# Attention into a gated feed-forward chain on one core: softmax sums turned once and spread by way of DRAM, last keys in one product

## The chip, the cores and the metric

The kernel runs on one core of one Trainium2 chip. The metric is the device time of one execution in microseconds. The time given is the median of several executions, and one further execution was profiled.

## The reference

```
scores = q @ k^T / sqrt(64)                   # 4 batches, 8 heads, 576 keys and queries, width 64
thresh = max(scores) - tau
scores = where(scores >= thresh, scores, -1e9)
attn   = exp(scores - max); attn /= sum(attn) + 1e-9
x      = attn @ v, heads side by side          # 2304 x 512
x      = (sigmoid(x @ w_gate) * (x @ w_val)) @ w_out      # 512 -> 1536 -> 512
h      = x @ w_in; out = (h * cos(h)) @ w_out2            # 512 -> 2048 -> 512
```

All in float32. Products are made on TensorE in float32r from a rounded high part and a rest, three matmuls (high by high, high by low, low by high) for one product.

## The kernel before

**Tiling.** Two heads make a pair; there are 16 pairs, four for each batch. A pair has nine score tiles of 128 queries by 576 keys: four for each head (`order`, line 566), and one that holds the last 64 queries of both heads. For one tile (`Queries.tasks`, line 589, with the key letters of the order lines): S, the scores on TensorE; M, the extreme of each row on VectorE (line 690); Y, the threshold, one column on VectorE (`threshold`, line 572); E, the exponential on ScalarE; K, the mask on VectorE, which also adds up each row into one column of the pair's `sums` tile (line 698); T, four 128x128 transposes to put keys on partitions (line 710), and t, one transpose for the last 64 keys of both heads (line 718). Each transposed tile is then split for the value product: H or h copies the rounded high part out of PSUM on ScalarE, and L or l takes the rest on VectorE (`low`, line 650); the table `LOWS` may give the rest to GpSimd by way of a copy (C, G) or to TensorE by a subtraction (N, n) and ScalarE (O, o).

**Value products.** `Values` (line 723) has four tasks V for each pair, two blocks of queries (256 and 320 columns) by two heads. The weights hold the high and low half of v side by side, so that 128 columns of weights give both. Each takes ten matmuls: high and low for four chunks of 128 keys, and high and low for the last keys, `LT`, which has both heads on its partitions (line 765). A "shared" one takes fifteen and needs no folding. The others are folded: F copies half of the result on ScalarE, A adds it into `x32` on VectorE.

**The sums.** `finish_pair` (line 779): p adds 1e-9 to the nine columns of `sums` (ScalarE), I inverts them (VectorE). For each of two blocks, R spreads four columns over 256 columns on GpSimd (`widen`), B transposes them on TensorE, two or three transposes of 128 columns (`spread`, line 806), so that each partition gets the factors of its head along the queries, and U multiplies x by them on VectorE from PSUM (`scaled`, line 815), with two more of 64x64 in the second block.

**After that.** D stores x to DRAM, X and x split it for the feed-forward stage (lines 839 and 840), and P are the first feed-forward products of batches 0 to 2 for half of the inner width (`groups`, line 863); their results are copied (e) to one of three `st` tiles and stored (g). They fill TensorE between the attention's tasks.

**Order.** The table `ORDER` gives a line of letters for each engine, in which each letter takes the next task of its kind; each engine's queue runs in that order. `WHERE` says on which engine some kinds run for each pair. The feed-forward stage that follows is laid out by the planner (`Plan.put_out`) without a table.

Of the kernel before, what the change touches and what calls it, by code (L numbers as in the profile page):

```python
# [19 lines left out]
P = 128  # L20
# [6 lines left out]
NT = 9  # L27
# [35 lines left out]
    ACT=(
        "JZQJQQwEEH6EHhEswHQOEh6HEFwCEHHHFhhEsHhEOQHEOpHh6EOEwaHHCE6FHZEOwhhEoo6HEFHHwHCEhhEHFhopEHHEOOh6wHEEsaHEF6HE"
        "OhhwoHEHHHEFZeHhh6EFHhEpOEHheewOEEFC6HFHwZEHeEhOXeh6EHEaHHehHEFhHEepwheHHEOhe6EHwEeHC6aEEFHChEHheEeHHHQFHEhF"
        "hEHpheEHheCHEEeFHCEFCsHhEhECHeeHHHEEFhhHpFHEheheECHEeEHFHCEEFHZehOEEHCheHHHEhhHFpeHEhEhFeHEEeFHCHEEFHChheEEH"
        "CeFHHCHEEHhhFpeHhEhECHeFHCHEFEZHChEEheHCeHHHEFhEhHehFpHEHehEEeHFCHEFEHChheEHEZFHHHEehhCHEeFhHphECEHeeHEEFCHF"
        "CHEhhEeHCEHHHEFhhHCeEhHEpFHhECEeFHHEFECHhhEEHCHHXHeEhhEHhpeFHCEEHhFeHECEHFCFEHhhEeHCeEHHHEehhEHFhpFHECheHEEe"
        "HFHCEFHEChEheEHZeHHHEeEhHFhhpFHEHehEHEeCHFEaEHChhEHCEFeHCHHEhheEHFhHEephECHeEEHCFHeEEFHChECHhEeHHHFHEhhehHbp"
        "FHheFFXeX"  # L70
    ),
    DVE=(
        "jzqjqqMYM4KY5KMLMYYKLlKM45YMlKYLKMAYMKLYLl4lKMYMKlY5AKMlIYMYKK4U5MLYMKAYUMK4Y5MKYLKMAYM4YLLKllKLMYMIYA5KKlMU"
        "YMKYLK4M5LYAMUKYlKM4YLMKYLLLKA5MlLYlKMAlMIYYKKlMYM45YKAUKMAYLMUYK45KlMlMLYKYKLMLYlLMAKlYLKIlM4Y5LKlMYUMYK4K5"
        "LMYMYKKAUMlYMKLlYKLLLMMYAYLlKlALlMIYKKlMUMYLKYMAYKAKUMMYlYKKlMYMLLYLKKlALAMIYlLKlMYlKMUYMYKKLAMYMYKKAUMYlMYK"
        "KlMYLLLKMLAlYlMLlKYlIKAMLYMYUKKALMMYYKKAUMlMlYKYKMAYMLYLKKLllAMLIlMlYUKYKAMLYMYKAKUMMlYYKKlMMLLLYKYlAlKLMIlA"
        "YLKMLlMUYYKKLMAYMKAYUKMllMYYKLKAMLLYLMYKllKlALMIMYlYKKMYUMYLKKAMAUMYYlKKlMMYYKLLLKAllMMYlYKKLILMlAYMYKUKMALY"
        "MKAYUKMlMYlKYKMLLMYLKYllKLIlMAMLYYKKlMAUMYKYKAMAYULMlYKlKMMYYKLLLMYKllLKAMlYALKIlMYMKYUKLAMMYKYAUKMYlMKlYKLM"
        "MYYLLLKKLllAMIlAYLKMLlMYYKUKLMYMAYKUKlMlMYYKKAMLLYMllKYLKMALYlMIYlKKUMYMKYKLAMMYYKKAUMlYMYKlKLLLMAYLllKLlIAL"
        "lAUAUx"  # L80
    ),
    POOL=(
        "ZJ7jqz7cGJjqR7RGs7Xx7zcJQqRGj7R7XxcJzjQR7RqG7x7zscJjQRq7R7sGXZGcxzqJRjGRGZGzGcXJjxQRqGRGscGJzXxQqRjsRGcGXxZG"
        "QzGqRJGRjGGzXxJcGRsQqRjGGscQqGzRRJGGjGcsGZGQqRJzRGZjGscGQXxxXJRqGRGxzjGXscGZxzQJqRGRGcsGjRQJzRqGjGZcGGRRzGGc"
        "GGRRXxXxx"
    ),
# [193 lines left out]
def pool1(n):  # L280
    return 0.03 + n / 943
# [1202 lines left out]
```

## Time and profile before

| what | us |
|---|---|
| median of 3 runs | 1146.27 |
| lowest and highest | 1146.10, 1146.92 |
| profiled execution, own time | 1143.7 |
| its span, first to last instruction | 1141.9 |

TensorE is busy for 97% of the span, VectorE 78%, ScalarE 62%, GpSimd 35%. The attention stage ends on TensorE with the last product L393 before 415.40 us, where the first product of the feed-forward stage begins. The page's slices say how busy an engine is; whether it waits is read from the windows and waits.

### The profile page before, as it was taken

Reading aid. Unit: us, or ns where it says so; the run is one execution under the profiler, and the core shown is the slowest. Engines: PE = TensorE matmul, PEld = TensorE weight load, DVE = VectorE, ACT = ScalarE, POOL = GpSimd, SP = SyncE. Lnnn points to the kernel's source line nnn. Section 1 sums busy time; section 2 is a strip of 40 time slices with the busy share of each in tenths; the row PEclk is TensorE's granted clock in tenths of the full one; section 3 lists DMA queues with packets and bytes.
Section 4 is the critical chain, followed back from the end, with each engine's and each line's share of the span. In section 5 each row is a group of like instructions: output and inputs, shape, how many; then the busy total and the mean of one; then the engine's idle time right before and its main releaser. Section 6 shows DMA issues by size and latency. Waiting matters only on the chain. (4 is left out here: it accounts for less than half of the span.)

```text
span 1141.9 us, 17082 instructions
## 1 busy us (share of the span) xinstructions
PE 1110.0 (97%) x5986; PEld 951.7 (83%) x5986; DVE 889.4 (78%) x1691; ACT 709.4 (62%) x1322; POOL 403.3 (35%) x338
## 2 busy tenths in 40 slices
PE   7889899999999999999999999999999999999998
PEld 6678798988899878988888888878888888888887
DVE  7899999999999848597335989989566777757664
ACT  6778788888787845565313555567754654676551
POOL 4656676876886425352002644430000000000000
PEclk8899999999999999999999999999999999999999
DMA  7444344553353148485102888995333433735421
GB/s 193 123 121 148 110 149 121 163 150 115 94 142 121 58 151 286 162 329 188 55 1 74 306 326 300 347 332 183 122 111 111 148 111 111 274 115 185 145 74 73
DMA packets 64100, 183.55 MB, mean 161 GB/s; under 512 B 8336, under 2 KB 8592, under 8 KB 56080
## 3 DMA queue, kind: packets, MB, share of 16 engines
q1 hardware_dynamic: 63856, 182.15, 47.7%
q8 instruction: 47, 0.77, 0.3%
q10 hardware_dynamic: 160, 0.33, 0.1%
q14 instruction: 37, 0.30, 0.1%
HBM read 131.07 MB, written 51.38 MB: 160 GB/s over the span
## 5 line engine op out<-in xcount | busy, mean ns | idle before, releaser
L690 DVE TENSOR_REDUCE sm<-s 128x1 f32<-128x576 f32 x144 | 107.5, 751 | 7.2 <-PE s L684 6.2
L1072 DVE TENSOR_TENSOR g<-g,g 128x512 fp32r<-128x512 f32 x118 | 93.9, 799 | 20.0 <-ACT g L1069 18.9
L1069 ACT ACTIVATE g<-g 128x512 fp32r<-128x512 f32 x118 | 73.8, 628 | 55.6 <-DVE g L1108 52.4
L698 DVE SCALAR_TENSOR_TENSOR p<-s,sm,p 128x576 f32<-128x576 f32 x128 | 103.0, 812 | 6.4 <-ACT p L695 4.6
L684 PE MATMUL s<-kk,qh 128*128 128x288 f32 x320 | 98.8, 326 | 6.7 <-DVE p L698 4.9
L695 ACT ACTIVATE p<-s,sm 128x576 f32<-128x576 f32 x128 | 94.7, 746 | 13.7 <-DVE sm L690 12.9
L1100 PE MATMUL h<-x,w 128*128 128x256 f32 (+1 forms) x304 | 101.3, 333 | 0.0
L1101 PE MATMUL h<-x,w 128*128 128x256 f32 (+1 forms) x304 | 101.3, 333 | 0.0
L1099 PE MATMUL h<-x,w 128*128 128x256 f32 (+1 forms) x304 | 101.3, 333 | 0.0
L1335 PE MATMUL o<-w,g 128*128 128x512 f32 x256 | 99.8, 390 | 0.0
L1336 PE MATMUL o<-w,g 128*128 128x512 f32 x256 | 99.7, 389 | 0.0
L1337 PE MATMUL o<-w,g 128*128 128x512 f32 x256 | 99.6, 389 | 0.0
L641 ACT ACTIVATE PT<-t 128x512 fp32r<-128x512 f32 (+1 forms) x160 | 85.7, 557 | 21.1 <-PE t L714 19.4
L684 PE MATMUL s<-kk,ql 128*128 128x288 f32 x320 | 91.8, 303 | 0.9 <-DVE ql L504 0.9
L356 POOL TENSOR_TENSOR w<-wt,w 128x512 fp32r<-128x512 f32 x30 | 40.4, 1356 | 134.9 <-ACT w L352 134.8
L714 PE MATMUL t<-ident,p 128*128 128x128 f32 x512 | 79.8, 282 | 7.3 <-DVE PT L652 3.0
L714 PEld LDWEIGHTS t<-ident,p 128*128 128x128 f32 x512 | 62.9, 144 | 17.6 <-DVE PT L652 3.5
L1273 PE MATMUL h<-form,w 128*128 128x512 f32 x192 | 75.2, 392 | 0.9 <-ACT h L1242 0.9
L684 PEld LDWEIGHTS s<-kk,qh 128*128 128x128 f32 x320 | 62.6, 196 | 15.4 <-issue 5.1
L1275 PE MATMUL h<-form,w 128*128 128x512 f32 x192 | 74.7, 389 | 0.0
L1274 PE MATMUL h<-form,w 128*128 128x512 f32 x192 | 74.7, 389 | 0.0
L661 POOL TENSOR_TENSOR PT<-praw,PT 128x512 fp32r<-128x512 f32 x47 | 60.6, 1289 | 37.2 <-ACT praw L656 17.3
(188 smaller groups left out, 3341.8 us busy)
## 6 DMA issues: line engine op xcount, KB each, us to landing
w<-wd SPq DMA_DIRECT2D x48, 1024.0 KB, 4.8
wd<-stage SPq DMA_DIRECT2D x48, 512.0 KB, 4.5
gd<-st SPq DMA_DIRECT2D x64, 256.0 KB, 3.4
wraw<-in_moe_w_out_dram SPq DMA_DIRECT2D x28, 512.0 KB, 5.0
raw_k<-in_k_dram SPq DMA_DIRECT2D x30, 304.0 KB, 4.7
raw_q<-in_q_dram SPq DMA_DIRECT2D x30, 288.0 KB, 4.4
wraw<-in_moe_w_in_dram SPq DMA_DIRECT2D x16, 512.0 KB, 5.3
early<-gd SPq DMA_DIRECT2D x7, 1024.0 KB, 6.0
```

The costliest lines, as they stand in the source:

```text
L684: nc.tensor.matmul(s[:, half, 0:HALF], qq[:, off:off + P], kk[:, k0:k0 + HALF], start=(i == 0), stop=(i == len(mms) - 1),)
L690: nc.vector.tensor_reduce(self.sm()[:, 0:1], self.s()[:, :, 0:HALF], axis=AX.XY, op=ALU.min)
L695: nc.scalar.activation(self.e, self.s()[:, :, 0:HALF], AF.Exp, bias=self.sm()[:, 0:1], scale=-1.0)
L698: nc.vector.scalar_tensor_tensor(self.e, self.s()[:, :, 0:HALF], self.sm()[:, 1:2], self.e, op0=ALU.is_le, op1=ALU.mult, accum_out=self.su ...
L714: nc.tensor.matmul(tp[:, c * P:(c + 1) * P], self.pn[:, k0:k0 + P], ident, is_transpose=True, start=(c == 0), stop=(c == 3))
L1072: nc.vector.tensor_tensor(g()[:, 1, 0:n], g32()[:, 0:n], f32(g()[:, 0, 0:n]), op=ALU.subtract)
L1099: nc.tensor.matmul(o, w_hi, x(0, c), start=begin, stop=False, **late)
L1100: nc.tensor.matmul(o, w_hi, x(1, c), start=False, stop=False, **late)
L1101: nc.tensor.matmul(o, w_lo, x(0, c), start=False, stop=c == KC - 1, **late)
L1335: nc.tensor.matmul(o(), hi, w_hi, start=i == 0, stop=False)
L1336: nc.tensor.matmul(o(), hi, w_lo, start=False, stop=False)
L1337: nc.tensor.matmul(o(), lo, w_hi, start=False, stop=i == len(parts) - 1)
```

## The change

Totals of tasks, counted in the order lines before and after:

| kind | engine | before | after |
|---|---|---|---|
| B transposes of sums (tasks; transposes) | TensorE | 32; 80 | 16; 16 |
| D four transposes into a score tile | TensorE | 0 | 15 |
| matmuls of V (shared tasks) | TensorE | 665 (5) | 606 (6) |
| n subtraction for last keys | TensorE | 4 | 0 |
| Y threshold | VectorE; ScalarE | 144; 0 | 67; 77 |
| l and h, last keys' rest and high part | VectorE; ScalarE | 92; 96 | 160; 160 |
| U multiplication of x | VectorE; GpSimd | 32; 0 | 3; 13 |
| R | GpSimd; SyncE | 32; 0 | 0; 64 loads, and 16 stores r |
| x low split of x | VectorE; GpSimd | 1; 15 | 4; 12 |
| X high split of x | ScalarE; GpSimd | 4; 12 | 7; 9 |

- The nine columns of sums go through one transpose (9 rows of 128), p and I work on 9 partitions, and the inverses are stored to DRAM in query order (r). Four loads (R) read them back, each row of one head to 64 partitions, 512 or 64 columns, into a tile `bc`. One multiplication of 128x576 replaces four.
- The last 64 keys: `LT` becomes one tile for each head, with the high part on the 64 partitions of the head and the rest on the other 64, so that one matmul over 128 partitions adds both; the values of these keys lie on both halves (`_values`). Each pair of tiles has now two copies h and two rests l of 64 partitions by 128 columns instead of one of 128 by 128.
- `FILL` puts groups of four transposes ("D") after the scores of some of the first 27 tiles; they write into a part of the score tile that nothing reads.
- All order lines, `LOWS`, `SHARED` and `WHERE` are new. `LOWS_L` and `BITS` are not used after it.

```diff
 ORDER = dict(
     PE=(
-        "SSTSSTtSTTNStVSTSTVtSTtSNTSTNtSNVBTSTSVTBSNttnSnTVSTTSVtTStnSTTNNtSTBSVTSVSTBNttSnTSVTTPStPTSVPTtPSNPTtPSNSB"
+        "SSDDDDSTSDTNDDSTtStDTVNSSTDTNSNNStTVtTSNSDtTVTBSStTVTSStTVSTTSNNDtTDSVNtSTDTtSNSBVTtVTSSTTDDStNSTTVNNPtSPTPS"
...
-LOWS_L = (
-    "VVVV TTTV VTVV VVVV VVVV VVVV VVVV VVVV VVVV VVVV VVVV VVVV VVVV VVVV VVVV VVVV "
...
+    Z="APPAPPPAPPPAAPPA", z="DPPPPPPPPPPPPPPP", s="APPAPPPPPPPPPAPP", X="PPAPAPPPPPPAAAAA", x="PPPPPPPPPPPPDDDD", U="PPPPPPPPPPPPDPDD",
...
+FILL = (
+    "311210010 010000002 010011000 000000000 000000000 000000000 000000000 000000000 "
...
+    rd = dpool.tile([NP, 2 * SM + P], F32, name="rd")
...
+    def threshold(n, engine):
         sm = sms[n]()
-        nc.vector.tensor_scalar(sm[:, 1:2], sm[:, 0:1], off, None, op0=ALU.add)
+        if engine is nc.scalar:
+            engine.activation(sm[:, 1:2], sm[:, 0:1], AF.Identity, bias=off)
+        else:
+            engine.tensor_scalar(sm[:, 1:2], sm[:, 0:1], off, None, op0=ALU.add)
+
+    def filler(s):
+        for _ in range(4):
+            nc.tensor.transpose(s()[:, 1, HALF:HALF + P], ident, ident)
...
+            def stacked(i, q0, n):
+                def parts():
+                    own, other = (LT[i]()[64 * k:64 * k + 64, q0:q0 + n] for k in (i, 1 - i))
+                    return Halves(own, other)
+                return parts
...
                 if h:
-                    ev.append((turn_l, tl, lambda: tl()[:, 0:P], LT, lambda: LT()[:, :, q0:q0 + P], P, [0, 1]))
+                    ev += [(turn_l, tl, lambda i=i: tl()[64 * i:64 * i + 64, 0:P], LT[i], stacked(i, q0, P), P, [i])
+                           for i in range(2)]
...
-            parts.append((8 + h, LT[:, 0, 0:n], LT[:, 1, 0:n]))
+            parts.append((8 + h, [LT[:, 0:n]]))
...
+        def turn_sums():
+            nc.tensor.transpose(tr()[0:9, 0:P], sm()[:, 0:9], ident)
+
         def more():
-            nc.scalar.activation(sm()[:, 0:9], sm()[:, 0:9], AF.Copy, bias=1e-9)
+            nc.scalar.activation(rs()[0:9], tr()[0:9, 0:P], AF.Copy, bias=1e-9)
 
         def inverse():
-            nc.vector.reciprocal(sm()[:, 0:9], sm()[:, 0:9])
...
+            nc.vector.reciprocal(rs()[0:9], rs()[0:9])
+
+        def along(h, tail):
+            row, to = (rd[pair.p:pair.p + 1, SM * h:SM * h + SM], slice(0, SM))
+            if tail:
+                row, to = rd[pair.p:pair.p + 1, 2 * SM + SL * h:2 * SM + SL * h + SL], slice(SM, S)
+            nc.sync.dma_start(bc()[64 * h:64 * h + 64, to], row.to_broadcast([64, to.stop - to.start]))
+
+        turned = task("PE", 0.107, "B", turn_sums, *pair.masks, uses=[sm, tr])
...
+        def scaled():
+            x = x32[:, c]
+            engine.tensor_tensor(x, x, bc(), op=ALU.mult)
```

## Rows read from the trace of the kernel before

**Rows 1.** Windows: stretch, length, busy us (and instructions) by engine, TensorE clock, DMA share, GB/s.

```profile
10.00:40.00 30.00, 21.38 (x110) 17.74 (x111) 25.66 (x61) 23.66 (x43) 19.91 (x13) 0.77 0.69 185
40.00:142.00 102.00, 90.08 (x565) 77.93 (x564) 94.27 (x220) 79.03 (x161) 64.85 (x58) 0.95 0.41 122
142.00:415.40 273.40, 270.84 (x1817) 243.28 (x1815) 250.13 (x652) 216.50 (x449) 191.27 (x170) 1.00 0.40 119
415.40:1142.00 726.60, 719.99 (x3457) 605.44 (x3455) 515.60 (x753) 385.48 (x664) 125.92 (x88) 1.00 0.51 181
```

**Rows 2.** Timeline of TensorE: start us, us, engine, line, operation, tiles, shapes.

```profile
255.01 0.28 PE L775 MATMUL v<-PT,vn 128*128 128x256 f32 x1
255.13 0.28 PE L774 MATMUL v<-PT,vn 128*128 128x256 f32 x1
...
409.35 0.31 PE L774 MATMUL v<-PT,vn 128*128 128x320 f32 x1
409.50 0.31 PE L775 MATMUL v<-PT,vn 128*128 128x320 f32 x1
...
414.37 0.38 PE L813 MATMUL t<-ident,wide 128*128 128x128 f32 x2
414.59 0.27 PE L813 MATMUL t<-ident,sums 128*128 128x128 f32 x1
414.61 0.48 PE L391 MATMUL m<-xs_a,w 128*128 128x512 f32 x1
414.93 0.39 PE L392 MATMUL m<-xs_a,w 128*128 128x512 f32 x1
415.16 0.40 PE L393 MATMUL m<-xs_a,w 128*128 128x512 f32 x1
```

**Rows 3.** Groups by line and form, VectorE, 142 to 416 us: busy us, mean ns | idle before.

```profile
L652 DVE TENSOR_TENSOR PT<-t,PT 128x512 fp32r<-128x512 f32 x50 | 34.4, 689 | 2.5 <-ACT PT L641 1.8
L575 DVE TENSOR_SCALAR sm<-sm,taus 128x1 f32<-128x1 f32 x100 | 19.7, 207 | 1.0
L652 DVE TENSOR_TENSOR LT<-t,LT 128x128 fp32r<-128x128 f32 x46 | 12.7, 279 | 2.1 <-ACT LT L641 1.9
L817 DVE TENSOR_TENSOR x<-t,x 128x256 f32<-128x256 f32 x24 | 10.1, 421 | 1.3 <-PE t L813 0.5
L652 DVE TENSOR_TENSOR LT<-t,LT 64x64 fp32r<-64x64 f32 x24 | 5.2, 218 | 0.5 <-ACT LT L641 0.3
L821 DVE TENSOR_TENSOR x<-t,x 64x64 f32<-64x64 f32 x24 | 5.2, 217 | 0.2
```

**Rows 4.** Groups by line and form, ScalarE, 142 to 416 us.

```profile
L641 ACT ACTIVATE LT<-t 128x128 fp32r<-128x128 f32 x46 | 12.6, 277 | 14.1 <-PE t L721 13.8
```

**Rows 5.** Groups by line and form, GpSimd, 142 to 416 us.

```profile
L506 POOL TENSOR_TENSOR vn<-raw_v,vn 128x640 fp32r<-128x640 f32 x11 | 17.3, 1573 | 0.0
L801 POOL TENSOR_SCALAR wide<-sums 128x256 f32<-128x256 f32 x24 | 9.8, 410 | 27.4 <-DVE sums L791 14.3 <-DVE sm L575 6.6 <-PE t L813 3.4
```

**Rows 6.** DMA issues: tiles, queue, count, KB each, median us to landing.

```profile
raw_q<-in_q_dram SPq DMA_DIRECT2D x2, 112.0 KB, 3.8
taus<-in_tau_dram SPq DMA_DIRECT2D x1, 0.5 KB, 2.6
```

**Rows 7.** Timeline of ScalarE and VectorE: sums ready and last addition, two pairs.

```profile
240.77 0.21 ACT L788 ACTIVATE sums<-sums 128x9 f32<-128x9 f32 x1
251.05 0.49 DVE L754 TENSOR_TENSOR x<-v,half 64x320 f32<-64x320 f32 x1
...
406.32 0.20 ACT L788 ACTIVATE sums<-sums 128x9 f32<-128x9 f32 x1
414.34 0.50 DVE L754 TENSOR_TENSOR x<-v,half 64x320 f32<-64x320 f32 x1 [2.04 <-ACT half L749]
```

**Rows 8.** Waits of SyncE's queue, whole span: us in total, times, longest.

```profile
SPq L889 <- ACT st L886: 97.0, 29, 8.8
```

**Rows 9.** Groups by line and form, VectorE, 0 to 440 us.

```profile
L1072 DVE TENSOR_TENSOR g<-g,g 128x512 fp32r<-128x512 f32 x3 | 4.2, 1393 | 0.0
```

More of the change, by code (lines that the diff above doesn't have):

```diff
@@ L67 @@
[L67 to L70, printed above, removed]
+        "JZQJQQwYEEJHEYHEYO6HhhwEhQYHEh6aOEHEHHOOOwhhHEYYEHahO6hhJhHEYYEwHpCah6HYEEYwHChahh6EHYEsHHHEOOwhhHEJEO6hhHEa"
@@ L729, in __init__ @@
             self.shared = SHARED[4 * pair.p + 2 * blk + h] == "S"
-            self.PT, self.LT = pair.PT[blk, h], pair.LT[blk]
+            self.PT, self.LT = pair.PT[blk, h], pair.LT[blk][h]
             self.bank = bank = bank_v()
-            pv = task("PE", products(n, 15 if self.shared else 10), "V", self.product, *pair.ready[blk, h],
+            pv = task("PE", products(n, 14 if self.shared else 9), "V", self.product, *pair.ready[blk, h],
                       pair.v_done, pvs[0], uses=[bank, self.PT, self.LT, pair.vb])
@@ L762, in product @@
             o = self.bank()[0:64 + 64 * h if self.shared else P, 0:n]
-            parts = [(4 * h + c, PT[:, 0, c, 0:n], PT[:, 1, c, 0:n]) for c in range(4)]
-            parts.append((8 + h, LT[:, 0, 0:n], LT[:, 1, 0:n]))
-            for z, (slot, hi, lo) in enumerate(parts):
-                vn = self.pair.vn.rearrange("p j a d -> p (j a d)")
+            vn = self.pair.vn.rearrange("p j a d -> p (j a d)")
+            parts = [(4 * h + c, [PT[:, 0, c, 0:n], PT[:, 1, c, 0:n]]) for c in range(4)]
+            parts.append((8 + h, [LT[:, 0:n]]))
+            steps = []
+            for slot, halves in parts:
                 if self.shared:
@@ L770, in product @@
                     w, w_lo = (vn[:, c0 + 64 * i:c0 + 64 * i + 64 + 64 * h] for i in range(2))
[L771 removed]
+                    steps += [(w, x) for x in halves] + [(w_lo, halves[0])]
                 else:
[L773 to L775 removed]
+                    steps += [(vn[:, 128 * slot:128 * slot + 128], x) for x in halves]
+            for z, (w, x) in enumerate(steps):
+                nc.tensor.matmul(o, w, x, start=z == 0, stop=z == len(steps) - 1)
     pvs, xs_of, x_ready, x_stored = [None], {}, {}, {}
@@ new lines, in inverse @@
+            nc.vector.reciprocal(rs()[0:9], rs()[0:9])
[5 more added lines that the diff above has]
+        turned = task("PE", 0.107, "B", turn_sums, *pair.masks, uses=[sm, tr])
+        inv = task("ACT", act(P), "p", more, turned, uses=[tr, rs])
@@ new lines, in finish_pair @@
+        inv = task("DVE", 0.2, "I", inverse, inv, uses=[rs])
+        kept = task("SP", 0.47, "r", lambda: nc.sync.dma_start(rd[pair.p].rearrange("(a n) -> a n", n=P), rs()[0:9]),
+                    inv, uses=[rs], moved=9)
+        spread = [task("SP", 0.47, "R", lambda h=h, tail=tail: along(h, tail), kept, uses=[bc], moved=(SL if tail else SM) // 2)
+                  for tail in range(2) for h in range(2)]
+        eu = either("U", pair.p)
+        engine = nc.vector if eu == "DVE" else nc.gpsimd
@@ L825, in finish_pair @@
+        def scaled():
+            x = x32[:, c]
+            engine.tensor_tensor(x, x, bc(), op=ALU.mult)
+        done = [task(eu, dve(S) if eu == "DVE" else pool2(S), "U", scaled, *spread, *pair.added[0], *pair.added[1],
+                     uses=[bc, pair.x], alone=eu == "DVE")]
         pair.done = done
@@ L1449, in _values @@
     for h in range(2):
-        out[:, SL * h:SL * h + SL, 8 + h] = t[:, h, SM:]
+        for i in range(2):
+            out[:, SL * i:SL * i + SL, 8 + h] = t[:, h, SM:]
     return out.reshape(NP, P, VW)
```

117 lines of the change are left out of this document (55 added, 62 removed).

## The prediction

> **What bounds the kernel now.** I read the windows first [rows 1]. After 142 us TensorE is busy for 270.84 of the 273.40 us that remain of the attention stage, and then for 719.99 of 726.60 us in the feed-forward stage. Between 142 and 415.4 us it idles for 2.6 us, all waits together. So in both of these stretches the end moves by what leaves TensorE's queue, as long as nothing else becomes slower than it. The nearest other engine there is VectorE with 250.13 of 273.40 us (91%); ScalarE has 216.50 and GpSimd 191.27. From 10 to 142 us it is different: TensorE idles for 8.6 + 11.9 = 20.5 us and its granted clock is 0.77 and 0.95, while VectorE is busy 119.9 of 132 us (91%). There VectorE, and the chain from one tile's scores over maximum, exponential and mask back to TensorE, sets the pace. The cut at 142 us is no accident of time: 100 of the 144 thresholds lie behind it [rows 3], so it stands close to the 45th score tile, and I count the new order lines up to and from that tile. "Early" and "late" mean these two halves of the attention stage.
>
> All durations are from the profiled execution: span 1141.9 us, its own time 1143.7 us. The median of the three runs is 1146.27 us, 2.6 us above it. I work out differences and take them off the median.
>
> **TensorE, late.** *Last keys in one product.* A value product over 256 columns steps 0.12 us from matmul to matmul (255.01 to 255.13), one over 320 columns 0.15 us [rows 2]. Each of the 46 value tasks that stand late loses one matmul, half of them of each width: 46 x 0.13 = 6.0 us. One shared task (15 matmuls) lay late before, none after: 5 more matmuls of 0.15, 0.7 us. *Sums turned by one transpose.* The three transposes of a pair's second half start at 414.37; the next product starts at 414.61, and its own first step is 0.32 us instead of 0.23 because it follows transposes [rows 2]. That is 0.24 + 0.09 = 0.33 us. Two of them I put at 0.26. One alone costs the last two terms, 0.02 + 0.09 = 0.11. So a pair saves 0.33 + 0.26 - 0.11 = 0.48 us, and 12 pairs lie late: 5.8 us. Sum late: 12.5 us.
>
> **VectorE, late.** Removed: 24 groups of multiplications, 24 x 0.42 + 24 x 0.22 = 15.3 us, and 55 thresholds of 0.21 moved to ScalarE, 11.4 us [rows 3]. Added: 44 splits of last keys, because each tile pair's is now two of 64 partitions; columns are as many, so I take 0.28 us each [rows 3], 12.3 us. No row shows VectorE writing its result to the other 64 partitions; ends are 0.28 and twice that, and I take 0.28, since the halved splits of 64 x 64 are priced by columns as well (0.22). Further 4 main splits at 0.69 (2.8), three multiplications of 576 columns and three splits of x that move here from GpSimd (together 4.8, from the 512-column row), one mask fewer (0.8). Sum: 26.7 + 0.8 - 12.3 - 2.8 - 4.8 = 7.6 us less. Load after: 242.5 us in a stretch of about 261 (93%).
>
> **ScalarE, late.** 44 more last-key copies at 0.28 and 54 thresholds at 0.21 (the row of 128x9 is the nearest) [rows 4, 7], less 4 copies: 216.5 + 12.3 + 11.3 - 2.4 + about 2 for three splits = 240 of 261 us (92%). That is full, but these durations overlap at their ends, so I leave it off the path; what it may cost is in the second rival.
>
> **GpSimd, late.** Gone are 24 spreads at 0.41 (9.8 us). The multiplication by 576 columns with two SBUF inputs is 1.573 x 576 / 640 = 1.42 us by the value split [rows 5]; with about nine of them late it is 12.7 us, and three splits of x leave. No net change; GpSimd idles 82 us of the stretch.
>
> **The way by DRAM.** SyncE issues one store and four loads per pair, and the loads wait for the store. A transfer of 0.5 KB lands after 2.6 us, one of 112 KB after 3.8 [rows 6]; with the four issues between, which no row prices (I put 0.4 us each), inverse to last row is 2.6 + 3.8 + 1.6 = 8 us. Its cover is the pair's own second half: in a middle pair the sums are ready at 240.77 and the last addition into x starts at 251.05, 10.3 us later; in the last pair it is 406.32 to 414.34, 8.0 us [rows 7]. So it hides, in the last pair with nothing to spare; if that cover is gone, the end pays what is over, 0 to 2 us. Queued behind the waiting loads on SyncE are loads for the next pair and stores of partial products. A store that is late holds one of three st tiles, and the next copy out of PSUM waits for it, and then TensorE for the bank. In the row of SyncE's waits it is SyncE that waits for ScalarE's copies, 97.0 us in 29 times [rows 8], so a store has room; I cost it at nothing.
>
> **Early.** Fifteen groups of four transposes are added on TensorE, 0.11 us for a transpose by the two that take 0.22 [rows 2], 6.6 us, in holes of 20.5 us [rows 1]. They cost nothing if they stay in holes and 6.6 us if they don't; the holes are three times as long, so I take nothing. VectorE's line up to the 45th tile has 24 last-key splits more (6.7 us), 3 + 3 main splits fewer with 1 added back (-5 x 0.69 = 3.4), 22 thresholds fewer (4.5), 8 groups of multiplications fewer (5.1), one split of queries and one mask more, one addition fewer (net +1.8): 4.5 us less. As VectorE is busy 91% of that stretch, most of it should come off: I take 3.5 us, with ends 0 and, if the tiles also come faster through TensorE, 10.
>
> **Feed-forward.** No product changes. The last value product is followed by two products instead of product, transposes, product; the multiplication of the last pair is one of 576 columns instead of three. Both chains, addition, multiplication, two splits, have the same number of steps; I take 0, ends -0.3 and +1.
>
> **Sum.** Late 12.5, less 1 for VectorE and ScalarE over 92% full: 11.5. Early 3.5. Together 15: 1146.3 - 15 = 1131 us.
>
> **The rivals.**
> *VectorE sets the pace late.* If a last-key split across partitions costs twice as much, or SyncE and GpSimd delay what it waits for, the stretch follows VectorE and not TensorE. With 0.28 us more for 44 splits its relief of 7.6 us turns into 4.7 us more work, and the late gain into nothing; at the plain price the late gain is 7.6. The middle of these and of an early gain of 0 to 3.5 is 6 us, but the nearer row is the plain price, so I take 7: 1139 us. For it: VectorE is at 91% already. Against: TensorE waits only 2.6 us today. A two-input operation on SBUF beside GpSimd took 1.393 us where 0.69 is usual [rows 3, 9], and four x splits and three multiplications of that kind come to VectorE at the end: 7 x 0.7 = 5 us of VectorE, which points the same way. The Trainium skill, page "SBUF — State Buffer", section "SBUF: two separate sides", says that this pair of ports is locked for a whole instruction and the loser blocks fully; by that rule these seven pay up to one GpSimd instruction each, and the row just named agrees with it.
>
> *Early gains more.* From 10 to 40 us the clock granted is 0.77, so 13.8 us lie at the lower level of 1.2 GHz, and from 40 to 142 us about 10 us [rows 1]. TensorE had idled before. If the added transposes keep the level at 2.4 GHz, work of these 24 us runs in half the time; half of the 12 us may lie on the chain: 6 us more, 1125 us. The Trainium skill, page "TensorE: Matmul & The Clock Gate", section "Part 1: The HAM clock gate", says that activity releases the throttle; by that the level would stay up. The rows of the clock fit it, but none shows what it is worth to a chain bound by VectorE, so it keeps a smaller chance than the sum.
>
> *GpSimd's queue stands behind the multiplication (slower).* The multiplication waits for the last addition and for the broadcast rows; behind it in line are the splits of queries, keys and copied scores that TensorE's next products need. GpSimd idles 82 / 11.4 = 7 us per pair. If the multiplication stood at the head for the whole 10.3 us between sums and last addition [rows 7], less those 7, each pair would lose 3.3 us: 11 x 3.3 = 36, less 15, 1167 us. It turns the sign from a wait of 7 + 15/11 = 8.4 us per pair on. Against it: the spreads stand in the same line today and idled it for 27.4 us in the late stretch [rows 5], while TensorE waited 2.6 us in all.
>
> *The saving turns into waits (no change).* The new lines could leave TensorE as many us of idle time as it lost in work, about 15; then 1146.
>
> **How the numbers follow.** Forecast 0.56; VectorE's pace 0.16; early gains more 0.16; GpSimd's queue 0.07; waits 0.05. The likeliest is 1131 us. The range goes to 1123 (late in full, early with the clock) and to 1140 (VectorE's pace); outside are the slower case, the unchanged one and a piece of each flank. This kernel's measurement can't tell less than about 0.2%, 2.3 us, from no change. Faster 0.88, same 0.05, slower 0.07.
>
> **What would show it.** Right: the feed-forward stage begins near 400 us instead of 415.4 and lasts 726 to 728 us; TensorE's idle time after the 45th tile stays under 6 us; the 45th tile comes 2 to 6 us earlier; value products have 9 matmuls. Wrong: idle time of TensorE in the late stretch released by VectorE's or ScalarE's splits of last keys (durations over 0.4 us); GpSimd idle before the multiplication by more than 5 us per pair with TensorE waiting after it; x splits waiting for a DMA of the broadcast tile; or a later 45th tile because the added transposes stand ahead of scores.

## The result and the profile after

The changed kernel is slower: 1157.4 us median of four runs (1156.13 to 1163.6) beside 1146.6 us for the kernel before (1146.1 to 1148.56), a ratio of 1.0102 with a 95% interval of 1.0064 to 1.014. The forecast was 1131 us. The profiled execution took 1157.61 us, its span is 1155.8 us; of before it was 1143.7 and 1141.9.

Where the 13.9 us of span came from is read by the order lines: the 46th extreme of a score tile (M) starts at 148.06 us where it started at 144.24 before, and the feed-forward stage begins at 426.97 instead of 415.40. So 3.8 us were lost up to the 46th tile, 7.8 us from there to the feed-forward stage, and 2.3 us in that stage (728.8 instead of 726.5). Windows of the changed kernel, columns as in [rows 1], cut at the 10, 40 and 142 us of those rows and at its own 46th tile and last attention product:

```profile
10.00:40.00 30.00, 23.93 (x149) 20.22 (x149) 23.49 (x49) 21.72 (x45) 14.96 (x11) 0.89 0.56 145
40.00:142.00 102.00, 88.21 (x553) 72.73 (x553) 95.95 (x206) 87.72 (x195) 70.62 (x54) 0.98 0.45 132
148.10:427.00 278.90, 269.14 (x1683) 225.32 (x1683) 259.90 (x594) 235.57 (x537) 191.03 (x151) 1.00 0.42 128
427.00:1155.80 728.80, 720.62 (x3457) 605.28 (x3455) 517.33 (x755) 386.71 (x665) 126.84 (x86) 1.00 0.51 180
```

The third line is the one to read against the same stretch of the kernel before, from its own 46th tile to its feed-forward stage:

```profile
144.30:415.40 271.10, 268.54 (x1798) 240.98 (x1796) 247.98 (x647) 214.25 (x444) 189.96 (x169) 1.00 0.40 120
```

TensorE has 115 matmuls less and is drawn busy for 0.6 us more, in a stretch that is 7.8 us longer: it now idles for 9.8 us instead of 2.6. Its weight loads for the scores wait for VectorE's mask, the last reader of a score tile (us in total, times, longest), in the kernel before and after the change:

```profile
PEld s L684 <- DVE p L698: 0.6, 2, 0.3
PEld s L730 <- DVE p L744: 7.9, 23, 0.7
```

VectorE went the other way. The forecast had it at 242.5 us, and it is busy for 259.90 of 278.90 (93%), 11.9 us more than before, with 53 instructions fewer. The groups of VectorE by line and form, 148 to 427 us, that answer to [rows 3]:

```profile
L698 DVE TENSOR_TENSOR PT<-t,PT 128x512 fp32r<-128x512 f32 x53 | 36.1, 687 | 1.4 <-ACT PT L687 0.6 <-POOL PT L707 0.2
L698 DVE TENSOR_TENSOR LT<-t,LT 64x128 fp32r<-64x128 f32 x92 | 26.6, 289 | 3.8 <-ACT LT L687 1.0
L845 DVE RECIPROCAL rs<-rs 9x128 f32<-9x128 f32 x12 | 11.2, 933 | 0.1
L602 DVE TENSOR_SCALAR sm<-sm,taus 128x1 f32<-128x1 f32 x45 | 9.2, 210 | 0.8
L865 DVE TENSOR_TENSOR x<-x,bc 128x576 f32<-128x576 f32 x2 | 1.4, 717 | 0.0
```

The reciprocal took 0.21 us on 128 partitions by nine columns before (12 in 2.5 us); on nine partitions by 128 columns it takes 0.93. The rests of the last keys have the duration that was forecast, 0.29 us, and still cost more than twice the forecast. That isn't in this view; it is in the timeline. VectorE in the kernel before, a rest of 128x128 between its neighbours (start, length):

```profile
244.13 0.68 DVE L652 TENSOR_TENSOR PT<-t,PT 128x512 fp32r<-128x512 f32 x1
244.72 0.28 DVE L652 TENSOR_TENSOR LT<-t,LT 128x128 fp32r<-128x128 f32 x1
244.92 0.75 DVE L690 TENSOR_REDUCE sm<-s 128x1 f32<-128x576 f32 x1
```

and in the changed kernel two rests of 64x128 behind a reciprocal:

```profile
279.83 0.93 DVE L845 RECIPROCAL rs<-rs 9x128 f32<-9x128 f32 x1
280.80 0.59 DVE L698 TENSOR_TENSOR LT<-t,LT 64x128 fp32r<-64x128 f32 x2
281.42 0.76 DVE L736 TENSOR_REDUCE sm<-s 128x1 f32<-128x576 f32 x1
```

Before, the rest starts 0.09 us ahead of its neighbour's end (244.13 + 0.68 = 244.81), and the next instruction 0.08 us ahead of its own end: it takes 0.20 us of the line. After, the first rest starts 0.04 us behind the end of the reciprocal, and the reduction 0.03 us behind the end of the rests: two take 0.62, and 0.12 more is lost ahead of them. Counted over the stretch where neither neighbour waits for another engine: of the 128x128 rests 36 of 38 overlap the instruction ahead of them in the kernel before, of the 64x128 rests (two in a row counted as one) 0 of 45 after, and 0 of 56 overlap the one behind them. A pair of score tiles paid 0.20 us for its last keys and pays about 0.75 now.

ScalarE and GpSimd, the groups that answer to [rows 4, 5], same stretch:

```profile
L687 ACT ACTIVATE LT<-t 64x128 fp32r<-64x128 f32 x92 | 24.9, 270 | 6.1 <-PE t L767 3.3 <-DVE LT L698 1.9
L600 ACT ACTIVATE sm<-sm,taus 128x1 f32<-128x1 f32 x54 | 15.4, 291 | 4.4 <-DVE sm L736 4.2
```

```profile
L865 POOL TENSOR_TENSOR x<-x,bc 128x576 f32<-128x576 f32 x9 | 12.8, 1427 | 2.3 <-DMA bc<-rd 2.3
```

A threshold takes 0.29 us on ScalarE, not the 0.21 of the forecast. GpSimd's multiplication takes 1.43 us, forecast 1.42, and stood waiting for its rows 2.3 us in all.

The early part, TensorE's timeline with the added transposes (L607), and the waits from 8 to 40 us (who waited for whom, us in total, times, longest):

```profile
11.99 0.66 PE L607 MATMUL s<-ident 128*128 128x128 f32 x4 [0.71 <-DVE sm L736]
13.47 0.68 PE L607 MATMUL s<-ident 128*128 128x128 f32 x4 [0.83 <-ACT p L741]
15.14 1.97 PE L607 MATMUL s<-ident 128*128 128x128 f32 x8 [0.99 <-DVE p L744]
```

```profile
DVE p L744 <- PE s L607: 3.3, 2, 2.0
ACT p L741 <- PE s L607: 1.7, 2, 1.2
DVE sm L736 <- PE s L607: 1.7, 1, 1.7
```

They write a part of the score tile that nothing reads, but they stand in order with the tile's readers: they wait for the extreme, the exponential and the mask of their tile, and these wait for them. The end of the stage, answering to [rows 7], from ScalarE, SyncE's issues, VectorE and TensorE:

```profile
421.66 0.27 ACT L842 ACTIVATE rs<-t 9x128 f32<-9x128 f32 x1 [0.28 <-PE t L839]
422.05 0.94 DVE L845 RECIPROCAL rs<-rs 9x128 f32<-9x128 f32 x1
...
424.74 2.44 SPq L851 DMA_DIRECT2D bc<-rd x4
...
427.10 0.49 DVE L800 TENSOR_TENSOR x<-v,half 64x320 f32<-64x320 f32 x1
...
429.19 0.76 DVE L865 TENSOR_TENSOR x<-x,bc 128x576 f32<-128x576 f32 x1 [0.88 <-DMA bc<-rd]
429.98 0.63 ACT L879 ACTIVATE xs_a<-x 128x512 fp32r<-128x512 f32 x1 [2.04 <-DVE x L865]
...
430.67 0.51 PE L1143 MATMUL h<-xs_a,w 128*128 128x512 f32 x1 [1.47 <-ACT xs_a L879]
```

From the sums on nine partitions to the landed rows it is 7.5 us (421.66 to 429.19), and 6.2 of them lie behind the end of the inverse, from where the forecast counted 8. But the last addition comes 5.4 us after the sums instead of 8.0, so the rest of the way shows, and TensorE waits 1.47 us for the split of the last x.

### The profile page after: what moved, and what is told of

It is laid out like the page before. It is cut to its first block, busy times and chain, and to the rows that moved or that the text cites. A ratio compares the mean times of both kernels' runs of the same rounds, so it can differ in the third digit from the quotient of the medians.

```text
span 1155.8 us, 17146 instructions
## 1 busy us (share of the span) xinstructions
PE 1115.2 (96%) x5919; PEld 936.1 (81%) x5919; DVE 906.5 (78%) x1623; ACT 742.4 (64%) x1460; POOL 409.4 (35%) x316
## 5 line engine op out<-in xcount | busy, mean ns | idle before, releaser
L1116 DVE TENSOR_TENSOR g<-g,g 128x512 fp32r<-128x512 f32 x118 | 98.3, 838 | 19.2 <-ACT g L1113 18.2
L741 ACT ACTIVATE p<-s,sm 128x576 f32<-128x576 f32 x128 | 93.4, 739 | 12.5 <-DVE sm L736 9.1
L822 PE MATMUL v<-PT,vn 128*128 128x256 f32 (+3 forms) x536 | 84.8, 301 | 1.2 <-DVE x L800 1.1
L707 POOL TENSOR_TENSOR PT<-praw,PT 128x512 fp32r<-128x512 f32 x48 | 64.1, 1335 | 52.5 <-ACT praw L702 39.4
L364 ACT ACTIVATE we<-wraw 128x512 f32<-128x512 f32 x68 | 45.6, 672 | 53.9 <-DMA wraw<-in_moe_w_out_dram 23.4
L760 PEld LDWEIGHTS t<-ident,p 128*128 128x128 f32 x512 | 59.7, 143 | 23.4 <-issue 6.9
L822 PEld LDWEIGHTS v<-PT,vn 128*128 128x128 f32 (+1 forms) x536 | 73.3, 185 | 4.4 <-DVE x L800 1.6
```

The source lines that it names most:

```text
L760: nc.tensor.matmul(tp[:, c * P:(c + 1) * P], self.pn[:, k0:k0 + P], ident, is_transpose=True, start=(c == 0), stop=(c == 3))
L822: nc.tensor.matmul(o, w, x, start=z == 0, stop=z == len(steps) - 1)
L1116: nc.vector.tensor_tensor(g()[:, 1, 0:n], g32()[:, 0:n], f32(g()[:, 0, 0:n]), op=ALU.subtract)
```

## The experiments

Ratios stand to the kernel before, run on the same chip. "Feed-forward begins" is the first product of that stage in the profiled execution: 415.40 before, 426.97 after. Two questions run through them: which engine sets the pace of the changed kernel, and what each part of the change costs there.

### Parts undone in the changed kernel

**No added transposes.**

```
- FILL = "311210010 010000002 010011000 ..."     PE line "SSDDDDSTSDT..."
+ FILL = "000000000 000000000 000000000 ..."     PE line "SSSTST..."
```

> The changed kernel without its 15 groups of added transposes; all else and every other order line as changed (1157.4 us). Theory 'the added transposes stand in the tile's chain' (they write the same score tile that maximum, exponential and mask read, and in the trace of the changed kernel the mask waits 3.3 us and the exponential 1.7 us for them): the tenth maximum comes at about 33 us instead of 36.65, and the time falls by 3 to 4 us, 1153 to 1154. Rival 'they hold TensorE's clock and that is worth more': the granted clock from 10 to 40 us falls from 0.89 to about 0.77 and the time rises or stays, 1157 to 1160.

1153.94 us, ratio 1.0067 (1.0043 to 1.0092), 3.5 us under the changed kernel. This interval and the changed kernel's own (1.0064 to 1.014) overlap, so the gain is read from the trace. The tenth extreme starts at 33.08 us; with the transposes it is 36.65, and 36.31 to 38.25 in the six other variants that keep them; in the kernel before and four variants of it that keep the last keys unsplit it is 33.36 to 34.96, and 37.05 in the one that splits them in the old order. The 46th moves from 148.06 to 143.53. So the transposes cost about as much as was lost early; the clock that they raise (0.89 from 10 to 40 us, 0.83 without them) doesn't pay for it. In the profiled execution most of the gain is lost again in the feed-forward stage (732.4 us instead of 728.8; the last section has the place).

**The reciprocal ahead of the transpose**, on 128 partitions by nine columns.

```
- turned = task("PE", 0.107, "B", turn_sums, *pair.masks, uses=[sm, tr])
- inv = task("DVE", 0.2, "I", inverse, inv, uses=[rs])           # reciprocal(rs()[0:9], rs()[0:9])
+ inv = task("DVE", 0.13, "I", inverse, *pair.masks, uses=[sm])  # reciprocal(sm()[:, 0:9], sm()[:, 0:9])
+ turned = task("PE", 0.107, "B", turn_sums, inv, uses=[sm, tr])
```

> The changed kernel with the reciprocals taken before the transpose, on 128 partitions of 9 columns, where the kernel before took 0.21 us for them, instead of 9 partitions of 128 columns, where the changed one took 0.93 us; number of tasks unchanged, only I stands earlier in VectorE's line. (The 1e-9 is left out; it is below the rounding of sums of at least 1.) Theory 'VectorE's own length is the bound': 16 x 0.72 = 11.5 us less on VectorE, time falls by 7 to 11 us, 1147 to 1150. Rival 'loss is in the order and the waits, the reciprocal is beside the path': falls by less than 3 us.

1148.79 us, ratio 1.0026 (1.0005 to 1.0047): 8.6 us less. The group of the reciprocal in this variant:

```profile
L845 DVE RECIPROCAL sums<-sums 128x9 f32<-128x9 f32 x12 | 2.6, 216 | 0.4
```

16 x (0.93 - 0.21) = 11.5 us of VectorE were taken away, and three quarters of them came off the time.

**All 144 thresholds on VectorE**, each right ahead of its mask.

```
- if YS[n] == "A":
+ if False:
- DVE "...llY5MKYKMllYLKll..."      ACT "...EYYEHa..."
+ DVE "...ll5MYKYKMllLYKll..."     ACT "...EEHa..."
```

> The changed kernel with all 144 thresholds on VectorE as before, each put right ahead of its mask, none on ScalarE. A threshold took 0.29 us on ScalarE and 0.21 on VectorE (0.13 from start to start). Theory 'VectorE is the bound': 77 x 0.13 = 10 us come to it, time rises by 5 to 10 us, 1162 to 1167. Rival 'ScalarE is the bound, or the mask waits for thresholds in ScalarE's line': 77 x 0.29 = 22 us leave ScalarE, time falls by 5 us or more, 1152 or less.

1184.4 us, ratio 1.0327 (1.0292 to 1.0362), 27 us more, where 5 to 10 were expected and 77 x 0.21 = 16 would be the price by durations. All 144 now stand right ahead of their own masks; of the 67 that were on VectorE already, 18 did so in the changed kernel (counted in the traces). VectorE is short of time; why so much, the run of the moved thresholds below shows.

**Last keys unsplit**, one rest and one copy for a pair of score tiles and two matmuls of 128 rows, as before the change.

```
- LT[i] = at.tile([P, 320]);      two rests of 64x128, parts.append((8 + h, [LT[:, 0:n]]))
+ LT = at.tile([P, 2, 320]);      one rest of 128x128, parts.append((8 + h, [LT[:, 0, 0:n], LT[:, 1, 0:n]]))
```

> The changed kernel with the last keys as in the kernel before: one copy and one rest of 128 partitions for each pair of tiles and two matmuls; the second of each two letters h and l is taken out of the lines, all else as changed. TensorE gets 64 matmuls more (64 x 0.13 = 8.3 us), VectorE and ScalarE lose 64 operations of 0.28 us each (0.2 from start to start on VectorE: 13 us). Theory 'VectorE is the bound': falls by 5 to 10 us, 1147 to 1152. Rival 'TensorE is the bound': rises by 5 to 8 us, 1162 to 1165.

1140.54 us, ratio 0.9942 (0.9923 to 0.9962): 16.9 us less, the largest part, though TensorE has a matmul more for each value product. The 64 copies taken from ScalarE are in this gain too. The feed-forward stage begins at 405.69.

**The three together.**

> The changed kernel with three parts undone together: no added transposes, reciprocals on 128 partitions ahead of the transpose (no 1e-9), last keys unsplit with two matmuls as before. What is left of the change: one transpose, the way by DRAM, one multiplication, thresholds partly on ScalarE, new order. Theory 'VectorE is the bound and the three add up': 1157.4 - 3.5 - 8.6 - 16.9 = 1128 us, and TensorE again idles under 4 us between 142 us and the end of attention. Rival 'TensorE takes over as the bound before the sum is reached': 1132 to 1137 us.

1128.06 us, ratio 0.9838 (0.981 to 0.9865). The parts add up: 1157.4 - 3.5 - 8.6 - 16.9 = 1128.4. Window from the 46th tile to the feed-forward stage:

```profile
135.02:397.23 262.21, 259.55 (x1728) 233.18 (x1727) 233.08 (x547) 220.70 (x492) 190.45 (x151) 1.00 0.45 137
```

VectorE is down to 89%, TensorE waits 2.7 us. What is left of the change here (sums turned once, DRAM, thresholds on ScalarE, new order) is worth some 18 us.

**The same with all thresholds on VectorE.**

> e5_three with all thresholds on VectorE, each ahead of its mask: 77 x 0.13 to 0.21 = 10 to 16 us more on VectorE, 22 us less on ScalarE. e5_three took 1128.06. Theory 'VectorE is the bound even there': 10 to 20 us slower, 1138 to 1148. Rival 'TensorE is the bound again, VectorE has room': 0 to 5 us slower, 1128 to 1133.

1144.13 us, ratio 0.9979 (0.9961 to 0.9996): 16 us more, 6.5 of them before the 46th tile. With all thresholds on VectorE, right ahead of their masks, what is left is worth 2 or 3 us; that place has a price of its own, as the moved thresholds show below.

### Work taken from one engine

**The changed kernel with 58 matmuls less** (every value product that isn't shared leaves out its product with the last keys).

```
+ steps = steps if self.shared else steps[:-1]
```

> The changed kernel with the last keys' one matmul left out of its 58 unshared value products: 58 x 0.13 = 7.5 us less on TensorE, the copies and rests of last keys still made. Theory 'after the change VectorE is the bound': under 2 us, 1156. Rival 'TensorE still is': 5 to 8 us faster, 1150 to 1152.

1160.05 us, ratio 1.0116 (1.0076 to 1.0157): nothing gained. From the 46th tile to the feed-forward stage TensorE idles for 11.9 us instead of 9.8, and VectorE is busy for 259.83 us, as long as in the changed kernel. TensorE doesn't pace the changed kernel.

**The kernel before with 59 matmuls less** (the value products that aren't shared leave out the last keys' high by low product).

```
  for z, (w, x) in enumerate(steps):
+     # the last of ten is left out, the ninth stops
```

> The kernel before with one matmul fewer in each of its 59 unshared value products (the low half of the last keys is left out): 59 x 0.13 = 7.7 us less on TensorE, nothing else touched. My prediction's ground, 'the late stretch ends when TensorE's line ends': 4 to 7 us faster, 1139 to 1142. Rival 'VectorE was as much the bound before already, TensorE only looks full': under 2 us, 1144 to 1146.

1144.71 us, ratio 0.9979 (0.9957 to 1.0002): between 4.9 us faster and nothing. The forecast priced 46 such matmuls at 6.0 us off the end. The window after 142 us:

```profile
142.00:414.60 272.60, 268.04 (x1770) 237.01 (x1769) 249.82 (x652) 216.37 (x449) 191.07 (x170) 1.00 0.39 119
```

Beside the third line of [rows 1] TensorE has 47 matmuls less and is still "busy" for 268 of 273 us. A matmul is drawn 0.28 to 0.39 us long while the next one steps 0.12 to 0.23 us behind it [rows 2], so a gap of up to some 0.15 us after each doesn't show as idle time. Counted by the median step of each form in the kernel before (0.234 us for 512 columns, 0.147 for 320, 0.133 for 288, 0.117 for 256 and 0.109 for a transpose of 128) the matmuls that start from 142 to 400 us fill 250 of 258 us before, 245 in this variant and 228 in the changed kernel. (The last transpose of a group steps only 0.03 us, but the product behind it then steps 0.08 longer, so each is taken at 0.109.) TensorE had room for some 8 us before where its busy time says 2, and has some 30 after the change.

**The kernel before with about 10 us less on VectorE** (the multiplications of x cover eight columns instead of 256 or 64).

```
- x = x32[:, c, 256 * blk:256 * blk + 256];  tr()[:, 0:256]
+ x = x32[:, c, 256 * blk:256 * blk + 8];    tr()[:, 0:8]
```

> The kernel before with the multiplications by the inverse sums cut to 8 columns each (64 instructions stay, x remains unscaled beyond them): about 0.25 us less for each of 32 of 256 columns and 0.06 for each of 32 of 64, 10 us less on VectorE, nothing else touched. Ground of the prediction 'TensorE is the bound late, VectorE early': 2 to 3 us faster, 1143. Rival 'VectorE is the bound in both halves': 6 to 10 us faster, 1136 to 1140.

1142.48 us, ratio 0.9974 (0.9955 to 0.9994): about 3 us.

**The kernel before with 77 thresholds on ScalarE**, in its old order.

```
- te = task("DVE", 0.122, "Y", threshold on VectorE)
+ te = task("ACT", ..., "Y", threshold on ScalarE)     # where the table of the changed kernel says so, behind the exponential
```

> The kernel before with the thresholds of the same 77 tiles on ScalarE as in the changed kernel, each right behind its exponential; the others stay where they are on VectorE, all else in the old order. VectorE loses 77 x 0.13 to 0.21 = 10 to 16 us, ScalarE gets 77 x 0.29 = 22 us. Theory 'the thresholds on ScalarE, and no part that the change names, make e5_three faster': 8 to 16 us faster than before, 1130 to 1138. Rival 'the old order holds each engine where it is, as in e8 and e9': within 3 us of before, 1142 to 1148.

1145.65 us, ratio 1.0002 (0.9981 to 1.0023): nothing. The mask now waits for ScalarE:

```profile
DVE p L706 <- ACT sm L578: 5.6, 14, 1.0
```

### Parts put into the kernel before

**The sums part alone**, old order, the multiplication on VectorE.

```
- widen (GpSimd), two or three transposes a block, scaled from PSUM: three multiplications
+ one transpose of nine columns, store r, four loads R, one multiplication of 128x576 by bc
```

> The kernel before with the sums part alone: reciprocals on 128 partitions (no 1e-9), one transpose, store and four loads, one multiplication of 576 columns on VectorE; all other letters in the old order. TensorE loses 64 transposes (7.7 us), VectorE 0.56 us a pair (9 us), GpSimd the spreads. Theory 'this part is a gain where the reciprocal is short': 4 to 8 us faster than before, 1137 to 1141. Rival 'the way by DRAM stalls a queue': same or slower, 1145 or more; U then shows waits for the broadcast tile in most pairs.

1186.36 us, ratio 1.0342 (1.0316 to 1.0368). Its waits after 142 us:

```profile
DVE x L825 <- DMA bc<-rd: 24.5, 9, 5.0
PEld t L723 <- DVE LT L661: 18.5, 11, 3.9
```

The multiplication stands in VectorE's line and waits there for its rows, up to 5 us, and the rests of last keys behind it come late for TensorE. The letters of the new tasks were placed by hand, so the size belongs to that placing; what it shows is what this wait costs when it stands in a line that others need. In the changed kernel it stands on GpSimd for most pairs.

**The last keys' part alone**, old order.

```
- one rest l and one copy h of 128x128 for a pair of score tiles, two matmuls
+ two rests l and two copies h of 64x128, one matmul over both halves
```

> The kernel before with the last-keys part alone: stacked tiles, one matmul instead of two, two copies and two rests of 64 partitions for each pair of tiles; the four subtractions on TensorE become rests on VectorE. Letters h and l doubled in place, all else in the old order. TensorE loses 64 matmuls (8.3 us), VectorE and ScalarE get 64 operations of 0.28 us (0.2 from start to start: 13 us on VectorE). Theory 'VectorE is bound next to TensorE': 5 to 12 us slower than before, 1150 to 1157. Rival 'TensorE is the bound': 4 to 8 us faster, 1137 to 1141.

1174.61 us, ratio 1.0241 (1.0219 to 1.0263): 28 us more. Window from 150 us to the feed-forward stage:

```profile
150.00:447.00 297.00, 279.27 (x1777) 236.63 (x1777) 273.13 (x702) 232.95 (x498) 191.65 (x171) 1.00 0.36 110
```

This is more than either side had expected. By durations 64 rests more are 18 us. By lost overlap a pair of tiles pays 0.55 us more, 64 x 0.55 = 35 us. The 28 us lie above the first, though 64 matmuls went away too; but 64 copies more on ScalarE and letters placed by hand are in them as well, so this run doesn't tell the two prices apart by itself.

### Is the lost overlap the price?

**Two rests, but each on its own half.** Head 0 is read and written on partitions 0 to 63, head 1 on 64 to 127; the two matmuls for them have 64 rows of weights.

```
- own, other = (LT[i]()[64 * k:64 * k + 64, q0:q0 + n] for k in (i, 1 - i))
+ return LT[i]()[64 * i:64 * i + 64, :, q0:q0 + n]
+ if z >= len(steps) - (3 if self.shared else 2): w, x = w[64 * h:64 * h + 64], x[64 * h:64 * h + 64]
```

> The changed kernel, but the two rests of a pair of score tiles are read and written on the same 64 partitions (head 0 on 0 to 63, head 1 on 64 to 127), high part and rest side by side again, with two matmuls over 64 rows of keys for them. The number of VectorE instructions and their shapes stay; TensorE gets 64 matmuls more. Theory of steps: in the changed kernel none of the 64x128 rests overlaps the instruction before or behind it in VectorE's line (each steps 0.31 to 0.32 us and takes about 0.11 from the one before), while the unsplit 128x128 rests step 0.20. If what stops the overlap is an operand that begins at partition 64, head 0's rests overlap again: 0.12 to 0.24 us less for each of 64 tile pairs, 8 to 15 us of VectorE, 6 to 11 of the time: 1146 to 1152. If it is the crossing of halves, both overlap: 23 to 30 us of VectorE, and some 10 to 13 of the time: 1144 to 1148. Theory of durations (a rest costs its 0.29 wherever it writes; only their number counts): no gain, 1155 to 1160.

1165.99 us, ratio 1.0165 (1.0141 to 1.0189): none of the three numbers. On VectorE the first theory holds. Of each two rests the first in VectorE's line is head 0's. Counted one by one where no neighbour waits for another engine, head 0's rest overlaps the instruction ahead of it in 21 of 26 cases, head 1's in 1 of 46. The instruction behind overlaps head 0's rest in 9 of 45 cases (34 of the others are head 1's rest) and head 1's in 5 of 45; these five are all additions into head 1's half of x. Shapes and durations are equal. The time tells nothing about it, because the edit brought a cost of its own. TensorE's timeline:

```profile
289.33 0.49 PE L823 MATMUL v<-LT,vn 64*128 64x256 f32 x2
289.76 0.50 PE L415 MATMUL m<-xs_a,w 128*128 128x512 f32 x1
```

The two matmuls of 64 rows take 0.43 us up to the next product; the one of 128 rows took 0.11 at the same place in the changed kernel (289.32 to 289.43). 46 late products by 0.32 us make 15 us more for TensorE. Whether that is what makes this variant slow isn't shown: TensorE is drawn busy for 279.67 us of 283.0, but by median steps its matmuls from 142 to 400 us fill 239 of 258.

**Thresholds on VectorE, one letter earlier.** All 144 on VectorE, as above, each one letter earlier; in the trace none stands right ahead of its own mask any more.

```
- DVE "...ll5MYKYKMllLYKll..."
+ DVE "...ll5YMYKKMllYLKll..."
```

> The variant with all 144 thresholds on VectorE (1184.4), with each threshold one letter earlier in VectorE's line, so that 111 of them no longer stand right ahead of their own mask. Theory of steps: a threshold right ahead of its mask steps 0.31 us there (all of them), because the mask needs its result and can't overlap it; with another instruction between, 0.13, as in the kernel before. 111 x 0.18 = 20 us less of VectorE: 1164 to 1172. Rival (the threshold costs its 0.21 wherever it stands, and the loss of 27 us came from somewhere else): 1181 to 1187.

1166.39 us, ratio 1.0175 (1.0151 to 1.0199): 18 us less than with the thresholds right ahead of their masks, by a change of order alone. A threshold right ahead of its mask, in the former variant:

```profile
300.45 0.20 DVE L602 TENSOR_SCALAR sm<-sm,taus 128x1 f32<-128x1 f32 x1
300.75 0.82 DVE L744 SCALAR_TENSOR_TENSOR p<-s,sm,p 128x576 f32<-128x576 f32 x1
```

and ahead of the mask of another tile, in this one:

```profile
300.54 0.21 DVE L602 TENSOR_SCALAR sm<-sm,taus 128x1 f32<-128x1 f32 x1
300.67 0.81 DVE L744 SCALAR_TENSOR_TENSOR p<-s,sm,p 128x576 f32<-128x576 f32 x1
```

The line moves on after 0.30 us in the one and 0.13 in the other, at equal durations. The medians are 0.31 us in the former variant, where all 144 stand ahead of their own mask, and 0.13 in this one. At 0.31 us, 77 thresholds are 24 us, and 49 of the other 67 had come to stand right ahead of their masks as well: this accounts for the 27 us.

**The three parts undone, thresholds one letter earlier** (25 of them; in the trace 22 stood right ahead of their own mask, and none does now).

> The variant with three parts undone (1128.1: no added transposes, reciprocal of nine columns, last keys unsplit), with 25 of the 33 thresholds that stand right ahead of their mask one letter earlier. Theory of steps: 25 x 0.18 = 4.5 us less of VectorE, two thirds or more of it off the time: 1123.5 to 1126. If VectorE isn't what paces this variant, or the instruction moved ahead was waiting anyway: 1127 to 1130.

1126.03 us, ratio 0.9822 (0.9797 to 0.9847). It lies at the end of what the steps gave, but its interval holds the 0.9838 of the variant without the move, so the two aren't told apart. Both beat the kernel before and the changed one.

## Why the prediction was wrong

**The first step failed: "the end moves by what leaves TensorE's queue".** It rested on TensorE's 270.84 busy us of 273.40 [rows 1]. That time is drawn from durations that overlap. 59 matmuls less moved the kernel before by 0.2%, with an interval that takes in zero and leaves out the 6.0 us that were forecast for 46 of them; 58 less gained the changed kernel nothing. So of TensorE's 12.5 us the matmuls' 6.7, right in their count (606, nine for a value product), did not come off the end; the transposes' 5.8 were not tried alone. What set the pace after the change was VectorE: TensorE idles for 9.8 us late instead of 2.6, and 11.5 us taken from VectorE alone gave 8.6 us of the time back.

**VectorE, late: forecast 7.6 us less, measured 11.9 us more** (247.98 to 259.90, each from its 46th tile). Two terms failed.
- *The reciprocal was not priced.* It stands in the diff with other operands, 9x128 instead of 128x9, and the forecast took it as unchanged. 12 late ones are 8.7 us of VectorE more, 16 are 11.5, and undoing all of them gave 8.6 us of the time back. The Trainium skill, page "VectorE: DVE Perf Modes", section "Walkthrough: the 8-slice pipeline in each mode", says that the reciprocal is an iterative division with a repeat count of 8; the trace agrees that columns are dear: 119 columns more took 0.725 us, 6.1 ns each, while the subtraction of 512 columns took 687 ns, 1.3 ns each.
- *The split of last keys was priced at 0.28 us a piece.* The prediction named the two ends, 0.28 and twice that, and took the lower. A pair of tiles pays 0.55 us more than before; the forecast had 0.28. So the dearer end was right, though the duration is the lower one: the price is the overlap lost on both sides. The Trainium skill, same page, section "Two Vector instructions with no wait between them", gives the rule: an instruction is held until every earlier one has finished if an input or the output starts in another group of 32 partitions than the last one in that memory did. The rows agree: rests that cross halves never overlap, and with each on its own half head 0's do (21 of 26) and head 1's, which start at partition 64, do not (1 of 46), as their neighbours start at partition 0 in nearly all cases. This rule would have made the first rival the likeliest case.

Relief was sized by durations as well: a threshold of 0.21 us or a multiplication of 256 columns of 0.42 gives back only its step in the line, 0.13 and 0.34 us (medians of the kernel before). 55 and 24 of these left late; at 0.08 each that is 6 us too much.

**Thresholds on ScalarE.** 0.29 us each instead of 0.21; 4 us more in 54. ScalarE's load came out below the forecast (235.57 of 278.90). The prediction says that its second rival holds what a full ScalarE may cost; that rival, the clock's, holds nothing of it. What the move is worth hangs on where the thresholds would stand otherwise: 16 us in the variant with three parts undone, against thresholds right ahead of their masks; in the changed kernel 27 us against those, and only 9 against thresholds one letter earlier; in the old order nothing.

**The way by DRAM.** The way itself stayed within the forecast (6.2 us from the end of the inverse, forecast 8). Its cover did not: 5.4 us between sums and last addition in the last pair, where the forecast used the 8.0 of the old order. The feed-forward stage is 2.3 us longer, of which 1.47 is TensorE's wait for the last split; the rest can't be told apart, as the unchanged stage takes 725.9 to 734.0 us in the variants. In middle pairs it hides; GpSimd's 2.3 us of waiting show it. The forecast put 0 to 2 us on this way, and 0 on the stage behind it.

**Early: forecast 3.5 us less, measured 3.8 more.** The transposes were put into TensorE's holes at nothing; the upper end, 6.6, was for TensorE's own time. The cost is in their order with the tile's readers, 3.5 us by the medians of the runs and 4.5 by the 46th tile, as the prediction's last line had it ("the added transposes stand ahead of scores"). The relief of VectorE that it took off early was eaten by the two dear terms: against the changed kernel the 46th tile starts 8.8 us earlier with the last keys unsplit (139.29), 2.3 with the other reciprocal (145.74) and 4.5 without the transposes (143.53).

**Rivals.** *VectorE sets the pace late* named the mechanism and the place; 1139 us came out because it held only one of the two dear terms, and at a price between its two ends. At the dear end, which was measured, it gives 1143 to 1146 by its own sum; with the reciprocal (8.6), the transposes (3.5) and the end (2.3) on top, which it did not have, that is 1157 to 1161; 1157.4 was measured. The seven operations that it feared beside GpSimd took 0.68 to 0.76 us each, with no delay. *Early gains more* fell: the clock did rise, to 0.89, and the tenth tile came 3.3 us later. *GpSimd's queue* fell with 2.3 us of waiting. *The saving turns into waits* holds for TensorE, 9.8 us idle late, but ends slower, not even.

**Open.** In the old order 7 to 10 us less on TensorE, on VectorE, or moved from VectorE to ScalarE gave 0 to 3 us each, so none of the three alone holds its pace; which lock of two does was not tried. In the new order what was taken from VectorE comes off part by part and adds up. Why the variant with each rest on its own half is 8.6 us slower than the changed kernel is open too. Why the last keys' 35 us of VectorE gave back 16.9 and the reciprocal's 11.5 gave 8.6 is not settled either; with the last keys undone TensorE has a matmul more in every value product, and idles for 3.9 us late instead of 9.8, so it may be the next bound.

## What to carry to other kernels

Price an instruction of a busy engine by its step, from its start to the start of the next, and look in the timeline for whether neighbours overlap. A busy share above 95% made of overlapping durations is no proof that this engine sets the end; a run that only takes work from it tests that. When an operation keeps its name but turns its operands, price it anew by its columns. Work put into an idle engine's holes costs nothing only if it is in no order with a tile that others read.

## What the runs showed of the hardware

- VectorE's instructions overlap by about 0.08 us when the next one isn't held; held ones start 0.01 to 0.03 us after the end. One lost overlap is about 0.11 us, more than half of a 0.20 us step.
- The reciprocal of 9x128 takes 0.93 us, of 128x9 0.21.
- A pair of 64-row matmuls between 128-row ones takes 0.43 us where one 128-row matmul of the same columns takes 0.11.
- A threshold of one column takes 0.29 us on ScalarE, 0.21 on VectorE.
- On VectorE a threshold right ahead of its own mask, which reads its result, steps 0.31 us in the median; ahead of anything else, in the run that moved it one letter, 0.13 us at the same duration.
- In the variant without added transposes TensorE's clock fell at the start of the feed-forward stage: 0.52 over 3.3 us, nearly all of them at the lower of its two levels, 1.2 GHz. TensorE had idled before that for 1.35 us at once and about 1.6 in all; it cost some 1.7 us. Windows of that variant:

```profile
422.30:425.90 3.60, 2.29 (x11) 1.53 (x9) 2.10 (x4) 1.66 (x3) 0.00 (x0) 1.00 0.35 123
...
427.70:431.00 3.30, 3.30 (x10) 2.54 (x9) 0.00 (x0) 0.00 (x0) 0.00 (x0) 0.52 0.78 210
```

In the changed kernel the same place idles about as long (2.19 us busy of 3.60) and keeps its clock. What tells the two apart was not tried.
